# A gated mix of decode attention and a SwiGLU block: the last 128 rows of w_down loaded in two pieces instead of eight

## The chip, the cores and the metric

The kernel runs on one core of a Trainium2 chip. The metric is the device time of one execution in microseconds (us), lower is better; times given are medians of several runs on the same chip.

## The reference

One token x of 512 values goes through two blocks, and a gate mixes their results. All tensors are bf16.

```python
g = sigmoid((x * gate_w).sum(-1))
# A: attention of 32 query heads over 8 cached K/V heads of 32768 positions x 128
q = (x @ wq).reshape(32, 128)                       # wq: 512 x 4096
p = softmax(q . k_cache[head // 4] * 128 ** -0.5)   # k_cache, v_cache: 8 x 32768 x 128
a = (p . v_cache[head // 4]).reshape(4096) @ wo     # wo: 4096 x 512
# B: feed-forward
b = (silu(x @ w_gate) * (x @ w_up)) @ w_down        # 512 x 1792, 512 x 1792, 1792 x 512
out = g * a + (1 - g) * b
```

K and V are 64 MiB each, and every byte is read once; the weights are 14 MB together.

## The kernel before

Everything is loaded through one DMA queue, in the order in which SP issues it: wq, w_gate and w_up, then for each of the eight K/V heads (groups) its K of 8 MiB and, one group behind, its V, then w_down, then wo. `page` is a tile of five pages of 32 KB per partition in which these loads land; K alternates between pages 0 and 1 and pages 1 and 2, V takes pages 3 and 4, and the last V takes pages 1 and 2. A load into a page waits until PE has read what was there. `sem_fill` counts PE's transposed pieces of K, 16 to a group; `sem_v_free` counts groups whose V has been used.

PE runs `emit_start` (the projections, the gate, the feed-forward's hidden vector), then the main loop over the eight groups, then `emit_end`. In a group PE transposes K in 16 pieces into PSUM (L364), DVE copies each to `ktT` (L735), PE multiplies it by the group's queries (L376), DVE takes the maximum, ACT the exponentials (L619), and PE multiplies them by V (L433) for the group before.

The feed-forward's hidden vector of 1792 values is made in `emit_start`. It lies in `trow`, in four strips of 448 on partitions 0, 32, 64 and 96; DVE spreads it to `tmask`, where a column has one value that is not zero (L706), and PE turns columns of `tmask` into partitions by multiplying with ones (L541). The first 1664 values become `tT`, 128 partitions x 13, and the last 128 become `tX`, 32 partitions x 4. The rows of w_down lie the same way: `wd` has 13 rows on each partition, in one load (L345), and the last 128 rows go to the first 32 partitions of page 0, four rows of 1 KB on each, side by side. L351 loads these in eight DMAs (`XQ` = 8): DMA q fills partitions q, 8 + q, 16 + q and 24 + q, so that four DMA engines (`XE` = 4) get one descriptor of 4 KB each. Page 0 held K of the last group, so SP first waits for all of K to be transposed (L348). Then it waits for the V of the last group but one to be used (L352) and issues wo in five pieces, of 16, 9, 4, 2 and 1 rows on each partition (L356).

In `emit_end` PE uses the last V, reduces, multiplies `tT` with `wd` and `tX` with the extra rows (`emit_strip`, L232), and then takes wo's pieces as they land: the first by `emit_strip`, the others by `emit_rows` (L243). DVE makes one bf16 row of the result (L788), and SP and ACT store half of it each.

GpSimd's program makes ones and index rows at the start and then only passes on semaphores.

Of the kernel before, what the change touches and what calls it, by code (L numbers as in the profile page):

```python
# [6 lines left out]
ALU = mybir.AluOpType  # L7
AX = mybir.AxisListType
BF16 = mybir.dt.bfloat16
# [3 lines left out]
def bass_gated_mix__gqa_block_cached__swiglu_ffn__decode_kernel(  # L13
# [14 lines left out]
    G = A_k_cache.shape[1]  # L28
# [4 lines left out]
    F = B_w_gate.shape[1]  # L33
    NOUT = A_wo.shape[1]
# [3 lines left out]
    FC = F // 128  # L38
# [37 lines left out]
    assert G % 2 == 0  # L76
    PAD = 768

    XQ, XE, FX = 8, 4, 4
    XP = XQ * XE  # L80
    FM = FC - XP * FX // 128
    FR = 128 * FM
    assert FR + XP * FX == F and FX == NSTRIP

    with ExitStack() as es:
        def S_(name):
            return es.enter_context(nc.semaphore(name))
# [9 lines left out]
        sem_ld_g = S_("s_ld_g")  # L97
        sem_ld_wd = S_("s_ld_wd")
        sem_ld_wx = S_("s_ld_wx")
        sem_ones = S_("s_ones")  # L100
        sem_dc = S_("s_dc")
        sem_pz = S_("s_pz")
# [42 lines left out]
        def T(name, shape, dt):  # L145
            return es.enter_context(nc.sbuf_tensor(name, shape, dt))
# [15 lines left out]
        qblk = T("qblk", [128, (G + 2) * STEP], BF16)  # L162
        qcur = T("qcur", [128, 2, 2 * HPG], BF16)
        tT = T("tT", [128, FM], BF16)
        tX = T("tX", [XP, FX], BF16)
        pad = T("pad", [128, PAD // 2], BF16)
        page = T("page", [128, NPG, PAGE], BF16)
        wd = T("wd", [128, FM, NOUT], BF16)
# [53 lines left out]

        wq_v = page[:, PG_Q, 0 : KC * H * DH].rearrange("p (c n) -> p c n", c=KC)
        wgu = page[:, PG_F, 0 : 2 * KC * F].rearrange("p (w c f) -> p w c f", w=2, c=KC)
        wx = page[0:XP, PG_A, 0 : FX * NOUT]
        wx_v = wx.rearrange("p (i n) -> p i n", i=FX)
        wo_v = page[:, PG_X, 0 : WOJ * NOUT].rearrange("p (j n) -> p j n", j=WOJ)
        qall = qblk[:, :].rearrange("p (g e c) -> p g e c", e=2, c=2 * HPG)

# [42 lines left out]
        with nc.Block("main") as block:  # L272
            @block.gpsimd
            def _(pool):
                pool.memset(ones_f[:, :], 1.0).then_inc(sem_ones, 1)
                pool.memset(ones_bf[:, :], 1.0).then_inc(sem_ones, 1)
                pool.memset(r_row[:, 0, 0:1], 0.0).then_inc(sem_r, 1)
                n, k = 1, 1
                while n < 128:
                    pool.wait_ge(sem_r, k)  # L280
                    pool.tensor_scalar(
                        r_row[:, 0, n : 2 * n], r_row[:, 0, 0:n], float(n), None, op0=ALU.add
                    ).then_inc(sem_r, 1)
                    n *= 2
                    k += 1
                pool.wait_ge(sem_r, k)
                pool.tensor_scalar(
                    r_row[:, 1, :], r_row[:, 0, :], -1.0, None, op0=ALU.mult
                ).then_inc(sem_r, 1)
                for g in range(1, G):  # L290
                    pool.wait_ge(sem_k[1], 16 * g)
                    if g > 1:
                        pool.wait_ge(sem_k[0], 16 * (g + 1))
                    else:
                        pool.wait_ge(sem_k1, 16)
                    pool.sem_inc(sem_k[1], 16)

            @block.sync
            def _(sp):
                def load_k(g):  # L300
                    lo = PG_A if g % 2 else PG_B
                    dst = page[:, lo : lo + NB, :].rearrange("p b (r d) -> p b r d", d=DH)
                    src = A_k_cache[0, g, :, :].rearrange("(p b r) d -> p b r d", b=NB, r=R)
                    if g > 1:
                        sp.wait_ge(sem_fill, UPG * (g - 1) + UPP)
                        sp.dma_start(
                            dst.rearrange("p b r d -> p (b r d)"),
                            src.rearrange("p b r d -> p (b r d)"),
                        ).then_inc(sem_k[0], 16)
                        return  # L310
                    for b in range(NB):
                        first = lo + b == PG_B
                        if g and first:
                            sp.wait_ge(sem_fill, UPP)
                        sp.dma_start(dst[:, b, :, :], src[:, b, :, :]).then_inc(
                            sem_k[0] if first else sem_k1 if g else sem_k[1], 16
                        )

                def load_v(g):
                    src = A_v_cache[0, g, :, :].rearrange("(p b r) d -> p b r d", b=NB, r=R)  # L320
                    if g == G - 1:
                        lo, sem = PG_L, sem_vl
                        sp.wait_ge(sem_fill, UPG * g + UPP)
                    else:
                        lo, sem = PG_V, sem_v
                        if g:
                            sp.wait_ge(sem_v_free, STEP * (g + 1))
                        else:
                            sp.wait_ge(sem_pe_h, 1)
                    sp.dma_start(  # L330
                        page[:, lo : lo + NB, :].rearrange("p b n -> p (b n)"),
                        src.rearrange("p b r d -> p (b r d)"),
                    ).then_inc(sem, 16)

                sp.dma_start(wq_v, A_wq.rearrange("(p c) n -> p c n", c=KC)).then_inc(sem_q, 16)
                for w, src in enumerate((B_w_gate, B_w_up)):
                    sp.dma_start(
                        wgu[:, w, :, :], src.rearrange("(p c) f -> p c f", c=KC)
                    ).then_inc(sem_f, 16)
                load_k(0)  # L340
                for g in range(1, G):
                    load_k(g)
                    load_v(g - 1)
                load_v(G - 1)
                sp.dma_start(  # L345
                    wd[:, :, :], B_w_down[0:FR, :].rearrange("(p j) n -> p j n", j=FM)
                ).then_inc(sem_ld_wd, 16)
                sp.wait_ge(sem_fill, UPG * G)  # L348
                rest = B_w_down[FR:F, :].rearrange("(e q i) n -> q e (i n)", q=XQ, i=FX)
                for q in range(XQ):  # L350
                    sp.dma_start(wx[q:XP:XQ, :], rest[q]).then_inc(sem_ld_wx, 16)  # L351
                sp.wait_ge(sem_v_free, STEP * G)  # L352
                src = A_wo.rearrange("(p j) n -> p j n", j=WOJ)
                for k, s in enumerate(sem_wo):
                    a, b = WO_CUTS[k], WO_CUTS[k + 1]
                    sp.dma_start(wo_v[:, a:b, :], src[:, a:b, :]).then_inc(s, 16)  # L356

            @block.tensor
            def _(pe):
# [103 lines left out]
                def emit_start():  # L463
# [70 lines left out]
                                    skip_group_check=True,  # L534
                                )
                    ins.then_inc(sem_pe_h, 1)
                    pe.wait_ge(sem_dve_tm, 1)
                    for c, n, lo, hi, m in ((M_T0, FM, 0, FR, 128), (M_T0 + FM, FX, FR, F, XP)):
                        tv = tmask[:, lo:hi].rearrange("p (m j) -> p j m", j=n)
                        for j in range(n):  # L540
                            ins = pe.matmul(  # L541
                                ps_m[0:m, c + j : c + j + 1],
                                tv[:, j, :],
                                ones_bf[:, 0:1],
                                start=True,
                                stop=True,
                            )
                    ins.then_inc(sem_pe_t, 1)
                    pe.wait_ge(sem_ps0, 1)
                    pe.wait_ge(sem_dve_tT, 2)  # L550
                    for n, sem in enumerate((sem_v_free, sem_red)):
                        c = M_P0 + HPG * n
                        pe.matmul(  # L553
# [16 lines left out]
                def emit_end():  # L570
# [5 lines left out]
                    pe.wait_ge(sem_ld_wd, 16)  # L576
                    for j in range(FM):
                        emit_strip(pe, wd, tT, j, j < NSTRIP, False)
                    pe.wait_ge(sem_ld_wx, 16 * XQ)
                    for j in range(FX):  # L580
                        emit_strip(pe, wx_v, tX, j, False, False, at=FM)

                    pe.wait_ge(sem_dve_oT2, 1)
                    pe.matmul(
# [46 lines left out]
            def _(dve):  # L631
                ndc = [0]

                def dchain(ins):
                    ins.then_inc(sem_dc, 1)
                    ndc[0] += 1
                    dve.wait_ge(sem_dc, ndc[0])

                dchain(dve.memset(qblk[:, :], 0.0))
                for t in pst:  # L640
                    dve.memset(t[:, :], 0.0).then_inc(sem_pz, 1)
                dve.wait_ge(sem_pe_d, 1)
# [32 lines left out]
                for par in range(2):  # L675
# [27 lines left out]
                        ALU.mult,  # L703
                    )
                )
                dve.tensor_tensor(  # L706
                    tmask.rearrange("p (s f) -> p s f", s=NSTRIP),
                    trow.unsqueeze(1).to_broadcast([128, NSTRIP, FS]),
                    strip_sel.unsqueeze(2).to_broadcast([128, NSTRIP, FS]),
                    ALU.mult,  # L710
                ).then_inc(sem_dve_tm, 1)
                dve.wait_ge(sem_pe_t, 1)
                dve.tensor_copy(tT[:, :], ps_m[:, M_T0 : M_T0 + FM]).then_inc(sem_dve_tT, 1)
                dve.tensor_copy(
                    tX[:, :], ps_m[0:XP, M_T0 + FM : M_T0 + FM + FX]
                ).then_inc(sem_dve_tT, 1)

                def emit_out(i, at):
                    dve.wait_ge(sem_red, i + STEP)
# [101 lines left out]
```

## Time and profile before

| | us |
|---|---|
| median of 3 runs | 350.08 (349.88 to 350.38) |
| profiled execution | 349.81 |
| its span, first to last instruction | 348.5 |
| PE busy | 262.4 |
| DVE busy | 186.3 |
| ACT busy | 33.4 |
| GpSimd busy | 2.8 |
| bytes read, rate over the span | 148.11 MB, 425 GB/s |

In the profile, L12 is line 12 of the kernel above, "out<-in" names what an operation writes and reads, and a row's numbers in parentheses or behind an x are counts of instructions. A DMA share of 1 means that all sixteen engines had a transfer open the whole time; a transfer's bytes are counted where it starts, so that short stretches are rough. "The chain that ended last" is followed back from the last instruction to what released each step.

### The profile page before, as it was taken

Reading aid. Unit: us, or ns where it says so; the run is one execution under the profiler, and the core shown is the slowest. Engines: PE = TensorE matmul, PEld = TensorE weight load, DVE = VectorE, ACT = ScalarE, POOL = GpSimd, SP = SyncE. Lnnn points to the kernel's source line nnn. Section 1 sums busy time; section 2 is a strip of 40 time slices with the busy share of each in tenths; the row PEclk is TensorE's granted clock in tenths of the full one; section 3 lists DMA queues with packets and bytes.
Section 4 is the critical chain, followed back from the end, with each engine's and each line's share of the span. In section 5 each row is a group of like instructions: output and inputs, shape, how many; then the busy total and the mean of one; then the engine's idle time right before and its main releaser. Section 6 shows DMA issues by size and latency. Waiting matters only on the chain.

```text
span 348.5 us, 8862 instructions
## 1 busy us (share of the span) xinstructions
PE 262.4 (75%) x3921; PEld 222.3 (64%) x3921; DVE 186.3 (53%) x228; ACT 33.4 (10%) x143; POOL 2.8 (1%) x15
## 2 busy tenths in 40 slices
PE   1355996799859981999469992999379973999384
PEld 1125986699459941997269942996279843995241
DVE  4044885499239921697139911895149920894101
ACT  1002000300030003000400003000400012000400
POOL 3000000000000000000000000000000000000000
PEclk9975798699889986799859987998859995898678
DMA  8999999999999999999999999999999999999996
GB/s 311 428 463 421 419 427 466 461 406 436 421 444 451 414 436 421 459 436 414 436 436 451 429 414 436 436 451 429 414 444 451 429 436 414 444 459 414 392 396 266
DMA packets 3970, 148.21 MB, mean 425 GB/s; under 512 B 474, under 2 KB 604, under 8 KB 892
## 3 DMA queue, kind: packets, MB, share of 16 engines
q1 hardware_dynamic: 3956, 148.11, 98.7%
q8 instruction: 6, 0.10, 0.1%
q10 hardware_dynamic: 8, 0.00, 0.0%
HBM read 148.11 MB, written 0.00 MB: 425 GB/s over the span
## 4 chain that ended last, share of the span: by engine, by line
DMA 58%; PE 36%; DVE 3%; issue 2%; SPq 1%; ACT 0%; DVEq 0%
DMA page<-in_A_k_cache_dram 46%; PE pst L364 26%; DMA page<-in_A_wo_dram 6%; PE ps_sc L376 6%; DMA page<-in_B_w_up_dram 6%; PE ps_o L433 2%; DVE ktT L735 1%; PE pst L528 1%; DVE ktT L706 1%; SPq L356 0%; PE ps_m L541 0%; PE ps_m L553 0%; DVE pmaxf L743 0%; DVE ktT L697 0%; PE ps_sc L243 0%
## 5 line engine op out<-in xcount | busy, mean ns | idle before, releaser
L735 DVE COPY ktT<-pst 128x2048 bf16<-128x2048 bf16 x128 | 153.6, 1222 | 65.3 <-PE pst L364 60.9
L364 PE MATMUL pst<-ident_f,page 128*128 128x128 f32 x1024 | 149.7, 302 | 38.4 <-DMA page<-in_A_k_cache_dram 35.4
L364 PEld LDWEIGHTS pst<-ident_f,page 128*128 128x128 f32 x1024 | 128.6, 156 | 42.5 <-DMA page<-in_A_k_cache_dram 35.9
L376 PEld LDWEIGHTS ps_sc<-qcur,ktT 128*128 128x128 bf16 x2048 | 64.0, 97 | 7.9 <-DVE ktT L735 6.8
L376 PE MATMUL ps_sc<-qcur,ktT 128*128 128x8 bf16 x2048 | 64.3, 166 | 6.1 <-DVE ktT L735 6.1
L433 PE MATMUL ps_o<-page,ET 128*16 128x512 bf16 x512 | 38.9, 472 | 5.7 <-DMA page<-in_A_v_cache_dram 5.7
L433 PEld LDWEIGHTS ps_o<-page,ET 128*16 128x16 bf16 x512 | 14.5, 107 | 26.2 <-issue 18.8
L619 ACT ACTIVATE ET<-ps_sc,nbias 128x128 bf16 x64 | 23.9, 555 | 53.3 <-DVE nbias L761 53.3
L612 ACT ACTIVATE acc<-ps_o 128x512 f32<-128x512 f32 x8 | 4.8, 597 | 220.0 <-PE ps_o L433 215.7
L753 DVE TENSOR_REDUCE gm<-ps_m 4x1 f32<-4x128 f32 x8 | 2.2, 279 | 39.3 <-PE ps_m L413 39.3
L619 ACT ACTIVATION_READ_ACCUMULATOR ET<-ps_sc,nbias 128x1 f32 x64 | 18.2, 285 | 0.0
L743 DVE TENSOR_REDUCE pmaxf<-ps_sc 128x4 f32<-128x512 f32 x16 | 11.0, 687 | 8.4 <-PE ps_sc L376 8.4
L490 PE MATMUL pst<-page,xT 128*1 128x512 bf16 x32 | 3.6, 627 | 8.9 <-DMA page<-in_A_wq_dram 8.9
L454 PE MATMUL ps_m<-sel,acc 128*128 128x4 f32 x64 | 8.4, 255 | 1.8 <-ACT acc L612 1.6
L454 PEld LDWEIGHTS ps_m<-sel,acc 128*128 128x128 f32 x64 | 7.7, 191 | 2.5 <-ACT acc L612 2.2
L417 PE MATMUL ps_m<-diag,ones_f 4*128 4x4 f32 x16 | 3.2, 268 | 6.9 <-DVE diag L757 6.9
L720 DVE RECIPROCAL rS<-ps_m 128x4 f32<-128x4 f32 x9 | 1.6, 183 | 12.1 <-PE ps_m L454 12.1
L417 PEld LDWEIGHTS ps_m<-diag,ones_f 4*128 4x128 f32 x16 | 2.7, 213 | 8.4 <-issue 8.4
L490 PEld LDWEIGHTS pst<-page,xT 128*1 128x1 bf16 x32 | 1.0, 115 | 10.7 <-issue 10.7
L670 DVE CAST ktT<-pst 128x1024 bf16<-128x1024 f32 x2 | 2.4, 1220 | 8.4 <-PE pst L490 8.4
L445 PEld LDWEIGHTS ps_m<-esum,ones_f 128*128 128x128 f32 x32 | 4.2, 190 | 3.5 <-issue 3.5
L445 PE MATMUL ps_m<-esum,ones_f 128*128 128x4 f32 x32 | 4.9, 258 | 0.0
(73 smaller groups left out, 49.4 us busy)
## 6 DMA issues: line engine op xcount, KB each, us to landing
page<-in_A_k_cache_dram SPq DMA_DIRECT2D x4, 4096.0 KB, 34.8
page<-in_A_wq_dram SPq DMA_DIRECT2D x1, 4096.0 KB, 13.4
page<-in_A_wo_dram SPq DMA_DIRECT2D x1, 2048.0 KB, 18.4
page<-in_B_w_gate_dram SPq DMA_DIRECT2D x1, 1792.0 KB, 17.1
page<-in_B_w_up_dram SPq DMA_DIRECT2D x1, 1792.0 KB, 20.9
wd<-in_B_w_down_dram SPq DMA_DIRECT2D x1, 1664.0 KB, 31.3
page<-in_A_wo_dram SPq DMA_DIRECT2D x1, 1152.0 KB, 20.8
page<-in_A_wo_dram SPq DMA_DIRECT2D x1, 512.0 KB, 21.5
```

The source lines that it names most:

```text
L364: ins = pe.transpose(pst[u % NST][:, k * 128 : (k + 1) * 128], kv[:, n * 128 : (n + 1) * 128], ident_f[:, :],)
L376: ins = pe.matmul(ps_sc[b][:, col : col + 2 * HPG], kt[:, k, e, :], qcur[:, e, :], start=(e == 0), stop=(e == 1),)
L417: pe.matmul(ps_m[:, M_B0 : M_B0 + HPG], ones_f[0:HPG, :], diag[:, :], start=True, stop=True,).then_inc(sem_b, STEP)
L433: ins = pe.matmul(ps_o[32 * c : 32 * c + RQ * HPG, :], ET[:, n : n + RQ, :].rearrange("p n h -> p (n h)"), v[:, k * RQ : (k + 1) * RQ, :], ...
L445: pe.matmul(ps_m[:, M_S0 : M_S0 + HPG], ones_f[:, :], esum[:, b, :], start=(b == 0), stop=(b == NB - 1),)
L454: ins = pe.matmul(ps_m[:, M_P0 : M_P0 + HPG], acc[:, q, :], sel4[:, q * HPG : (q + 1) * HPG], start=(q == 0), stop=(q == RQ - 1),)
L490: ins = pe.matmul(pst[0][32 * k : 32 * k + 1, t * QN : (t + 1) * QN], xT[:, c : c + 1], wq_v[:, c, n : n + QN], start=(c == 0), stop=(c == ...
L528: ins = pe.matmul(pst[1][32 * k : 32 * k + 1, w * 512 : w * 512 + FS], xT[:, c : c + 1], wgu[:, w, c, k * FS : (k + 1) * FS], start=(c == ...
L612: act.activation(part, ps_o[:, :], ACT.Copy).then_inc(sem_acc, STEP)
L619: act.activation(ET[:, b * R : (b + 1) * R, h], sc[:, h, bass.ds(bank, R)], ACT.Exp, bias=nbias[:, h : h + 1], scale=SCALE, accum_out=esum ...
L735: dve.tensor_copy(ktT[:, n % NKT, :], pst[n % NST][:, :].bitcast(BF16)).then_inc(sem_cp, 1)
L743: dve.tensor_reduce(pmaxf[:, b, :], sc, AX.X, ALU.max).then_inc(sem_d, 1)
```

## The change

The last 128 rows go in two loads (`XH` = 2) of sixteen partitions each, 0 to 15 and 32 to 47. In load h, DMA engine e (of four) fills partitions 32h + 4e + q for q = 0 to 3, with rows of w_down that lie 16 KB apart, so that at each q the four engines read neighbouring 4 KB. Partitions 16 to 31 lie between the two halves, so GpSimd clears the first 48 partitions of the page before the loads (new semaphore `s_wz`, on which SP's loads wait in place of `sem_fill`), DVE clears `tX`, which has 48 partitions now, and the matmul runs over all 48. The values of the hidden vector must follow the rows: DVE writes the last 128 columns of `tmask` once more, in two products that reorder them, behind a wait for the first product; PE makes `tX` in eight matmuls instead of four, and DVE copies it in two parts instead of one.

```diff
@@ -76,11 +76,13 @@
     assert G % 2 == 0
     PAD = 768
 
-    XQ, XE, FX = 8, 4, 4
-    XP = XQ * XE
-    FM = FC - XP * FX // 128
+    XH, XE, XQ, FX = 2, 4, 4, 4
+    XP = XE * XQ
+    XS = 32 * (XH - 1) + XP
+    FM = FC - XH * XP * FX // 128
     FR = 128 * FM
-    assert FR + XP * FX == F and FX == NSTRIP
+    assert FR + XH * XP * FX == F
+    assert XH * XP * FX <= FS
 
     with ExitStack() as es:
         def S_(name):
@@ -97,6 +99,7 @@
         sem_ld_g = S_("s_ld_g")
         sem_ld_wd = S_("s_ld_wd")
         sem_ld_wx = S_("s_ld_wx")
+        sem_wz = S_("s_wz")
         sem_ones = S_("s_ones")
         sem_dc = S_("s_dc")
         sem_pz = S_("s_pz")
@@ -162,7 +165,7 @@
         qblk = T("qblk", [128, (G + 2) * STEP], BF16)
         qcur = T("qcur", [128, 2, 2 * HPG], BF16)
         tT = T("tT", [128, FM], BF16)
-        tX = T("tX", [XP, FX], BF16)
+        tX = T("tX", [XS, FX], BF16)
         pad = T("pad", [128, PAD // 2], BF16)
         page = T("page", [128, NPG, PAGE], BF16)
         wd = T("wd", [128, FM, NOUT], BF16)
@@ -222,8 +225,8 @@
 
         wq_v = page[:, PG_Q, 0 : KC * H * DH].rearrange("p (c n) -> p c n", c=KC)
         wgu = page[:, PG_F, 0 : 2 * KC * F].rearrange("p (w c f) -> p w c f", w=2, c=KC)
-        wx = page[0:XP, PG_A, 0 : FX * NOUT]
-        wx_v = wx.rearrange("p (i n) -> p i n", i=FX)
+        wz = page[0:XS, PG_A, 0 : FX * NOUT]
+        wx = [page[32 * h : 32 * h + XP, PG_A, 0 : FX * NOUT] for h in range(XH)]
         wo_v = page[:, PG_X, 0 : WOJ * NOUT].rearrange("p (j n) -> p j n", j=WOJ)
         qall = qblk[:, :].rearrange("p (g e c) -> p g e c", e=2, c=2 * HPG)
 
@@ -294,6 +297,8 @@
                     else:
                         pool.wait_ge(sem_k1, 16)
                     pool.sem_inc(sem_k[1], 16)
+                pool.wait_ge(sem_fill, UPG * G)
+                pool.memset(wz, 0.0).then_inc(sem_wz, 1)
 
             @block.sync
             def _(sp):
@@ -345,10 +350,12 @@
                 sp.dma_start(
                     wd[:, :, :], B_w_down[0:FR, :].rearrange("(p j) n -> p j n", j=FM)
                 ).then_inc(sem_ld_wd, 16)
-                sp.wait_ge(sem_fill, UPG * G)
-                rest = B_w_down[FR:F, :].rearrange("(e q i) n -> q e (i n)", q=XQ, i=FX)
-                for q in range(XQ):
-                    sp.dma_start(wx[q:XP:XQ, :], rest[q]).then_inc(sem_ld_wx, 16)
+                sp.wait_ge(sem_wz, 1)
+                rest = B_w_down[FR:F, :].rearrange(
+                    "(h q e i) n -> h e q (i n)", h=XH, q=XQ, e=XE
+                )
+                for h in range(XH):
+                    sp.dma_start(wx[h], rest[h]).then_inc(sem_ld_wx, 16)
                 sp.wait_ge(sem_v_free, STEP * G)
                 src = A_wo.rearrange("(p j) n -> p j n", j=WOJ)
                 for k, s in enumerate(sem_wo):
@@ -534,20 +541,26 @@
                                     skip_group_check=True,
                                 )
                     ins.then_inc(sem_pe_h, 1)
-                    pe.wait_ge(sem_dve_tm, 1)
-                    for c, n, lo, hi, m in ((M_T0, FM, 0, FR, 128), (M_T0 + FM, FX, FR, F, XP)):
-                        tv = tmask[:, lo:hi].rearrange("p (m j) -> p j m", j=n)
-                        for j in range(n):
+                    pe.wait_ge(sem_dve_tm, XH)
+                    tv = tmask[:, 0:FR].rearrange("p (m j) -> p j m", j=FM)
+                    tx = tmask[:, FR:F].rearrange(
+                        "p (h m i) -> p i h m", h=XH, m=XP
+                    )
+                    cols = [(tv[:, j, :], 128) for j in range(FM)]
+                    cols += [(tx[:, i, :, :], XP) for i in range(FX)]
+                    for j, (lhsT, m) in enumerate(cols):
+                        for h in range(1 if m == 128 else XH):
                             ins = pe.matmul(
-                                ps_m[0:m, c + j : c + j + 1],
-                                tv[:, j, :],
+                                ps_m[32 * h : 32 * h + m, M_T0 + j : M_T0 + j + 1],
+                                lhsT if m == 128 else lhsT[:, h, :],
                                 ones_bf[:, 0:1],
                                 start=True,
                                 stop=True,
+                                skip_group_check=True,
                             )
                     ins.then_inc(sem_pe_t, 1)
                     pe.wait_ge(sem_ps0, 1)
-                    pe.wait_ge(sem_dve_tT, 2)
+                    pe.wait_ge(sem_dve_tT, 1 + XH)
                     for n, sem in enumerate((sem_v_free, sem_red)):
                         c = M_P0 + HPG * n
                         pe.matmul(
@@ -576,9 +589,10 @@
                     pe.wait_ge(sem_ld_wd, 16)
                     for j in range(FM):
                         emit_strip(pe, wd, tT, j, j < NSTRIP, False)
-                    pe.wait_ge(sem_ld_wx, 16 * XQ)
+                    pe.wait_ge(sem_ld_wx, 16 * XH)
+                    w = wz.rearrange("p (i n) -> p i n", i=FX)
                     for j in range(FX):
-                        emit_strip(pe, wx_v, tX, j, False, False, at=FM)
+                        emit_strip(pe, w, tX, j, False, False, at=FM)
 
                     pe.wait_ge(sem_dve_oT2, 1)
                     pe.matmul(
@@ -637,6 +651,7 @@
                     dve.wait_ge(sem_dc, ndc[0])
 
                 dchain(dve.memset(qblk[:, :], 0.0))
+                dchain(dve.memset(tX[:, :], 0.0))
                 for t in pst:
                     dve.memset(t[:, :], 0.0).then_inc(sem_pz, 1)
                 dve.wait_ge(sem_pe_d, 1)
@@ -703,17 +718,32 @@
                         ALU.mult,
                     )
                 )
-                dve.tensor_tensor(
-                    tmask.rearrange("p (s f) -> p s f", s=NSTRIP),
-                    trow.unsqueeze(1).to_broadcast([128, NSTRIP, FS]),
-                    strip_sel.unsqueeze(2).to_broadcast([128, NSTRIP, FS]),
-                    ALU.mult,
-                ).then_inc(sem_dve_tm, 1)
+                dchain(
+                    dve.tensor_tensor(
+                        tmask.rearrange("p (s f) -> p s f", s=NSTRIP),
+                        trow.unsqueeze(1).to_broadcast([128, NSTRIP, FS]),
+                        strip_sel.unsqueeze(2).to_broadcast([128, NSTRIP, FS]),
+                        ALU.mult,
+                    )
+                )
+                n = XP * FX
+                for h in range(XH):
+                    lo = F - n * (XH - h)
+                    at = FS - n * (XH - h)
+                    dve.tensor_scalar(
+                        tmask[:, lo : lo + n].rearrange("p (e q i) -> p e q i", e=XE, q=XQ),
+                        trow[:, at : at + n].rearrange("p (q e i) -> p e q i", e=XE, q=XQ),
+                        strip_sel[:, NSTRIP - 1 : NSTRIP],
+                        None,
+                        op0=ALU.mult,
+                    ).then_inc(sem_dve_tm, 1)
                 dve.wait_ge(sem_pe_t, 1)
                 dve.tensor_copy(tT[:, :], ps_m[:, M_T0 : M_T0 + FM]).then_inc(sem_dve_tT, 1)
-                dve.tensor_copy(
-                    tX[:, :], ps_m[0:XP, M_T0 + FM : M_T0 + FM + FX]
-                ).then_inc(sem_dve_tT, 1)
+                for h in range(XH):
+                    at = slice(32 * h, 32 * h + XP)
+                    dve.tensor_copy(
+                        tX[at, :], ps_m[at, M_T0 + FM : M_T0 + FM + FX]
+                    ).then_inc(sem_dve_tT, 1)
 
                 def emit_out(i, at):
                     dve.wait_ge(sem_red, i + STEP)
```

## The prediction

> **What bounds the kernel now.** I read the transfer summary first, then the chain that ended last, then the rate by stretch, then what the queue's issuer (SP) waits for. The summary (packets, MB, share of sixteen DMA engines) says that the transfers never pause:
>
> ```profile
> q1 hardware_dynamic: 3956, 148.11, 98.7%
> ```
>
> The chain's end shows what the last part waits for. Columns: start, duration, what.
>
> ```profile
> 315.62 1.23 DVE ktT L735
> 316.89 0.96 PE ps_sc L376 x32
> 317.85 5.28 PE ps_o L433 x64
> ...
> 324.47 21.67 DMA page<-in_A_wo_dram
> 346.14 0.04 issue
> 346.18 0.64 PE ps_sc L243 x12
> 346.82 0.02 issue
> 346.84 0.29 DVE res_row L788
> ```
>
> The last piece of A_wo is issued at 324.47 and lands at 346.14; behind it stand 0.64 us of matmuls, one copy and the store. PE's work ahead of it is over long before. So the end comes when the DMA engines have drained their queue, and an edit counts only if it changes how long the draining takes, or leaves the queue empty for a while. The rate by stretch (columns: length, busy time of PE, PEld, DVE, ACT and POOL, PE clock, DMA share, GB/s):
>
> ```profile
> 300.00:324.00 24.00, 22.98 (x396) 19.04 (x392) 16.83 (x17) 0.60 (x1) 0.00 (x0) 0.93 1.00 434
> 331.00:334.00 3.00, 1.90 (x20) 0.77 (x24) 0.00 (x0) 0.00 (x0) 0.00 (x0) 0.50 0.97 414
> 334.00:337.00 3.00, 3.00 (x44) 1.21 (x40) 0.00 (x0) 0.00 (x0) 0.00 (x0) 0.75 1.02 339
> 337.00:344.00 7.00, 4.73 (x62) 2.42 (x54) 0.98 (x5) 1.20 (x2) 0.00 (x0) 1.00 0.98 414
> ```
>
> One stretch stands out. From 334 to 337 the share is full (1.02, packets are open all the time) and yet 339 GB/s arrive instead of 434. What passes then follows from the issues (line, operation, count, KB each, us to landing):
>
> ```profile
> wd<-in_B_w_down_dram SPq DMA_DIRECT2D x1, 1664.0 KB, 31.3
> page<-in_B_w_down_dram SPq DMA_DIRECT2D x8, 16.0 KB
> page<-in_A_wo_dram SPq DMA_DIRECT2D x1, 2048.0 KB, 18.4
> ...
> 305.42 0.43 SPq L345 DMA_DIRECT2D wd<-in_B_w_down_dram  x1
> 315.34 5.07 SPq L351 DMA_DIRECT2D page<-in_B_w_down_dram  x8
> 323.14 2.24 SPq L356 DMA_DIRECT2D page<-in_A_wo_dram  x5
> ```
>
> The bulk of w_down, issued right after the last V pages, lands 31.3 us after its issue at 305.42, so near 336.7. The eight small loads stand behind it on the same queue and ahead of A_wo. The slow stretch is where those eight loads run out and A_wo begins. Lost there are (434 - 339) x 3 = 285 KB, or 285 / 434 = 0.66 us; against the neighbours at 414 it is 225 KB, 0.54 us. Since everything afterwards waits for the draining, this is on the path in full.
>
> **The change part by part.** *The loads.* Removed: eight loads of 16 KB, each of four rows of 4 KB to partitions eight apart. Added: two of 64 KB, each of sixteen rows to neighbouring partitions, four in a row for each of the same four parts of the source. The bytes are the same, 131 KB, and so is the number of 4 KB rows, 32. Six completion signals on each engine in use go; the trace does not price one, and the eight loads together can cost no more than the stretch they lie in. What can change is the 0.54 to 0.66 us of stall. Its bounds: a gain of the whole of it, 0.66 (0.95 if the 414 after it, seven us long and (434 - 414) x 7 / 434 = 0.32 us short, is its tail and not the price of smaller rows), and, since the trace does not show the new shape, a loss of the same size or of twice that. I take the gain of 0.66: of all loads these are the only ones that send four short rows to partitions far apart, and the only stretch after the start in which a full queue moves a fifth less than 434 is theirs. [...]
>
> [...]
>
> *The clearing.* GpSimd writes 48 partitions x 2048 columns of bf16 once all K tiles are transposed, and SP's two loads wait for it.
>
> ```profile
> L275 POOL MEMSET ones_f<- x1: 205/205/205, 0.7 to 0.7; 128x128 f32 x1
> L276 POOL MEMSET ones_bf<- 128x2 bf16 x1 | 0.1, 97 | 0.0
> SPq L356 <- PE ps_o L433: 2.7, 1, 2.7
> ...
> 329.34 0.58 ACT L619 ACTIVATE ET<-ps_sc,nbias 128x128 bf16 x1
> 332.10 5.30 PE L433 MATMUL ps_o<-page,ET 128*16 128x512 bf16 x64 [5.65 <-DMA page<-in_A_v_cache_dram]
> ```
>
> From 2 columns in 97 ns to 128 in 205 ns is 0.86 ns a column: 2048 columns take 1.9 us, or 1.0 if two are cleared at once. It begins where SP's wait ended, at 315.3, and if the last tile copy (to 316.84) held it up, it ends by 318.8. Two issues at 5.07 / 8 = 0.63 each make 320.1. Behind SP's new wait stand these loads and then A_wo's five, and A_wo isn't issued before 323.14, for it waits for PE (the 2.7 us above). So the clearing costs nothing; even 3 us more would only delay issues whose data cannot move before 334. If instead it held up the tile copy for 1.9 us, PE's matmuls and the exponentials behind it would come 1.9 later; they end at 329.9 and V's data at 332.1 is what PE then waits for: 2.2 us of cover. Nothing.
>
> *The start.* tX's own memset and its wait lie ahead of DVE's idle time. After the masked product DVE adds a wait and two small products, PE four matmuls, DVE one copy:
>
> ```profile
> 27.86 2.02 DVE L706 TENSOR_TENSOR ktT<-ktT,ident 128x1792 bf16<-128x1792 bf16 x1
> 29.94 1.17 PE L541 MATMUL ps_m<-ones_bf,ktT 128*128 128x1 bf16 x17 [4.16 <-DVE ktT L706]
> 31.23 0.14 DVE L714 CAST tX<-ps_m 32x4 bf16<-32x4 f32 x1
> L648 DVE CAST pmat<-ident_f 128x128 bf16<-128x128 f32 x1 | 0.3, 261 | 0.0
> L690 DVE TENSOR_SCALAR og_col<-g_col 128x1 f32<-128x1 f32 x1 | 0.1, 149 | 0.0
> ```
>
> A product over 64 columns lies between 149 ns (one column) and 261 ns (128 columns, reordered); two make 0.30 to 0.52, I take 0.40. PE: 4 x 1.17 / 17 = 0.28. The copy: 0.08 to 0.14. Together 0.8 us later into the main loop. The chain that ended last runs from here on PE and DVE up to 76.42, where K for group 2 is issued, so that issue comes 0.8 later:
>
> ```profile
> 76.42 23.80 DMA page<-in_A_k_cache_dram
> page<-in_A_wq_dram SPq DMA_DIRECT2D x1, 4096.0 KB, 13.4
> 4.00:20.00 16.00, 5.34 (x42) 2.55 (x42) 4.40 (x9) 0.17 (x1) 0.00 (x0) 1.00 0.98 419
> PE pst L364 <- DMA page<-in_A_k_cache_dram: 35.4, 6, 7.1
> ```
>
> In the first row 23.8 us pass from issue to landing of 8.39 MB, which need 8.39 / 0.434 = 19.3. So 4.5 us were queueing and start-up. The first load of all met an empty queue, and took 13.4 us for 4.19 MB, 10.0 at 419: start-up is at most 3.4. The queue therefore held 1.1 to 4.5 us of other work when this load was issued, and 0.8 fits below the lower bound. From the next group on PE waits for K itself (35.4 us in six waits), which swallows the shift. Cost nothing; with the cover gone it would be up to 0.8.
>
> *The end.* The same four matmuls take w_down's rest, now over 48 rows, and whatever they add lies ahead of a wait for A_wo of 1.09 us:
>
> ```profile
> 341.69 1.03 PE L232 MATMUL ps_sc<-page,O 128*1 128x512 bf16 x16 [1.09 <-DMA page<-in_A_wo_dram]
> ```
>
> Nothing.
>
> **Sum.** The profiled execution took 349.81 us, 348.5 of span and 1.3 around it; the median of the runs shown is 350.08, 0.27 above. 349.81 - 0.66 + 0 + 0 + 0 = 349.15; on the median's scale 349.4.
>
> **The rivals.** *Stall stays (B).* It would belong to the passage from w_down to A_wo, as all sixteen engines begin rows that are 32 KB apart. For it: such a beginning is slow once more, at the start of wq. Against it: the later pieces of A_wo have the same spacing and run at 414.
>
> ```profile
> 1.50:4.00 2.50, 0.00 (x0) 0.00 (x0) 1.57 (x2) 1.28 (x1) 1.99 (x7) 1.00 1.09 341
> ```
>
> Then nothing changes but a few signals: 350.0.
>
> *Stall grows (C), the slower side.* Each load now goes to sixteen partitions only, and each part of the source is read in 4 KB pieces 16 KB apart, where the eight old loads walked through 32 KB in order. If crowding at either side is what stalls, the place is the same stretch, 334 to 337, and the price another 0.66 (350.7) to 1.3 (351.4), middle 351.1; it counts as slower from a stall of 1.36 us on. Against it: the same 32 partitions' worth of rows and the same four sources at a time. [...]
>
> *The start's cover is too thin (D).* Should the queue hold less than the added 0.8 us at 76.4, the engines idle for the rest, at most 0.8: 350.9. Against it stands the lower bound of 1.1.
>
> **How the numbers follow.** About 0.2%, 0.7 us, is what a measurement of this kernel tells from no change. Forecast (A) 0.48, B 0.26, C 0.16, D 0.10. A runs from a gain of 0.54 to one of 0.95, so a bit over half of it, 0.28, lies beyond 0.7; with 0.02 of B faster is 0.30. Same: 0.20 of A, 0.22 of B, 0.02 each of C and D: 0.46. Slower: 0.14 of C, 0.08 of D, 0.02 of B: 0.24. With the spread of the runs A's own range is 349.0 to 349.7. The range 349.0 to 350.9 takes in A, B, D and C's lower end, and leaves out some 0.15.
>
> **What would show it.** In the changed profile: the stretch 334 to 337 at 414 or more; A_wo's last piece landing near 345.5 instead of 346.14 with the same 2.4 us behind it; SP's two issues done before 321 and A_wo's first issue still near 323; the loop's first transposes 0.8 us later, and K for group 2 landing within 0.3 us of 100.2. I am wrong if the slow stretch keeps its depth (B), deepens (C), or if it is gone and the time stays, which would mean that another engine's queue ended last.

## The result and the profile after

The changed kernel takes 349.19 us (349.06 to 349.53, 13 runs) against 349.96 (349.70 to 350.38, 13 runs): a ratio of 0.9978, with a 95% interval of 0.9969 to 0.9986, or 0.77 us less. Its profiled execution took 349.16, with a span of 347.8 (before: 349.81 and 348.5).

The rate by stretch of the changed kernel, in the same stretches as before:

```profile
331.00:334.00 3.00, 1.79 (x20) 0.75 (x24) 0.00 (x0) 0.00 (x0) 0.00 (x0) 0.50 0.95 408
334.00:337.00 3.00, 3.00 (x44) 1.21 (x40) 0.00 (x0) 0.00 (x0) 0.00 (x0) 0.65 1.02 435
337.00:344.00 7.00, 5.50 (x94) 2.83 (x90) 0.98 (x5) 1.20 (x2) 0.00 (x0) 1.00 0.98 413
```

The slow stretch is gone: 435 GB/s where it was 339, at the same full share of 1.02. Its neighbours are near where they were (408 and 413 instead of 414). The chain that ended last (start, duration, what) has moved by as much:

```profile
315.93 1.22 DVE ktT L765
317.20 0.96 PE ps_sc L383 x32
318.16 5.28 PE ps_o L440 x64
...
324.78 20.75 DMA page<-in_A_wo_dram
345.53 0.04 issue
345.57 0.29 PE ps_sc L246 x8
345.87 0.04 issue
345.90 0.27 PE ps_sc L246 x4
346.17 0.02 issue
346.19 0.29 DVE res_row L818
```

PE's steps around 317 are 0.31 us later than before and wo's last piece is issued 0.31 later, yet it lands 0.61 earlier, at 345.53 instead of 346.14. What follows the landing takes 2.3 us instead of 2.4. The timeline shows the clearing and the two loads:

```profile
315.69 1.80 POOL L301 MEMSET page<- 48x2048 bf16 x1 [311.70 <-PE pst L371]
317.52 1.48 SPq L358 DMA_DIRECT2D page<-in_B_w_down_dram  x2
323.45 2.24 SPq L363 DMA_DIRECT2D page<-in_A_wo_dram  x5
```

### The profile page after: what moved, and what is told of

It is laid out like the page before. It is cut to its first block, busy times and chain, and to the rows that moved or that the text cites. A ratio compares the mean times of both kernels' runs of the same rounds, so it can differ in the third digit from the quotient of the medians.

```text
span 347.8 us, 8869 instructions
## 1 busy us (share of the span) xinstructions
PE 260.8 (75%) x3925; PEld 220.6 (63%) x3925; DVE 186.6 (54%) x232; ACT 33.4 (10%) x143; POOL 4.6 (1%) x16
## 4 chain that ended last, share of the span: by engine, by line
DMA 64%; PE 33%; DVE 2%; issue 1%; SPq 1%; ACT 0%; DVEq 0%
DMA page<-in_A_k_cache_dram 52%; PE pst L371 24%; DMA page<-in_B_w_up_dram 6%; DMA page<-in_A_wo_dram 6%; PE ps_sc L383 5%; PE ps_o L440 2%; PE pst L535 1%; DVE ktT L722 1%; DVE ktT L765 0%; SPq L363 0%; PE ps_m L553 0%; PE ps_m L566 0%; DVE ktT L712 0%; DVE ktT L710 0%; PE ps_sc L246 0%
## 5 line engine op out<-in xcount | busy, mean ns | idle before, releaser
L371 PE MATMUL pst<-ident_f,page 128*128 128x128 f32 x1024 | 147.2, 299 | 39.5 <-DMA page<-in_A_k_cache_dram 38.2
L371 PEld LDWEIGHTS pst<-ident_f,page 128*128 128x128 f32 x1024 | 126.0, 154 | 43.9 <-DMA page<-in_A_k_cache_dram 38.8
L301 POOL MEMSET page<- 48x2048 bf16 x1 | 1.8, 1798 | 311.7 <-PE pst L371 311.7
```

The costliest lines, as they stand in the source:

```text
L371: ins = pe.transpose(pst[u % NST][:, k * 128 : (k + 1) * 128], kv[:, n * 128 : (n + 1) * 128], ident_f[:, :],)
```

## The experiments

Three sides of the new loads had to be told apart from each other and from the rest of the change: the loads are fewer (theory N), their source is read in another order (S), and they go to other partitions (P). All kernels are the changed one with a few lines edited, except one that is named; each is compared with the kernel before on the same chip. The pieces of code leave out the semaphores. A ratio is estimated from all executions of a kernel, so where these lie far apart it need not be that of the medians; a rate is that of one profiled execution.

**The eight old loads in the changed kernel.**

```diff
-rest = B_w_down[FR:F, :].rearrange("(h q e i) n -> h e q (i n)", h=XH, q=XQ, e=XE)
-for h in range(XH):
-    sp.dma_start(wx[h], rest[h])
+rest = B_w_down[FR:F, :].rearrange("(e q i) n -> q e (i n)", q=8, i=FX)
+for q in range(8):
+    sp.dma_start(page[q:32:8, PG_A, 0 : FX * NOUT], rest[q])
```

> The changed kernel with the eight old loads put back (four rows each, to partitions q, 8+q, 16+q, 24+q; its extra rows of w_down then stand on other partitions than the hidden vector's values). If the whole gain lies in the loads: about 349.96, ratio to before 1.000 (0.999 to 1.001), and 334 to 337 us back at about 340 GB/s. If the gain comes from another part of the change (the start, the clearing, where the clock or the code lies): ratio 0.998 and 334 to 337 at 430 or more.

Measured: 349.97, ratio 0.9999 (0.9990 to 1.0008). Its rate by stretch:

```profile
334.00:337.00 3.00, 3.00 (x36) 1.08 (x32) 0.00 (x0) 0.00 (x0) 0.00 (x0) 0.50 1.04 337
```

The whole gain lies in the loads; with the start, the clearing and the extra matmuls kept, the time is that of the kernel before (349.97 against 349.98 on the same chip).

**Eight loads to the new places.**

```diff
 for h in range(XH):
-    sp.dma_start(wx[h], rest[h])
+    for q in range(XQ):
+        sp.dma_start(wx[h][q:XP:XQ, :], rest[h, :, q, :])
```

> The changed kernel with its two loads cut into eight, of four rows each, every row to the same partition as in the changed kernel and from the same place. Theories P and S: no stall, ratio 0.998 (some 0.04 us of signals more), 334 to 337 at 425 or more. Theory N: the stall is back, ratio 1.000, 334 to 337 near 340.

Measured: 349.15, ratio 0.9978 (0.9969 to 0.9987), the same as the changed kernel (349.19, ratio 0.9978); the 0.04 us put for signals is not seen.

```profile
334.00:337.00 3.00, 3.00 (x32) 1.07 (x28) 0.00 (x0) 0.00 (x0) 0.00 (x0) 0.50 1.04 442
```

Theory N falls: eight loads of four rows, each row at the new place, took 349.15, two of sixteen 349.19.

**The source in plain order.**

```diff
-"(h q e i) n -> h e q (i n)"
+"(h e q i) n -> h e q (i n)"
```

> The changed kernel with the source taken in plain order: engine e reads 16 KB in one piece, the four engines 16 KB apart, as the old loads did with 32 KB (the rows then stand on other partitions than their values). Theories P and N: no stall, ratio 0.998, 334 to 337 at 430 or more. Theory S: the stall is back at least in part, ratio 0.999 to 1.000, 334 to 337 below 400.

Measured: 350.63, ratio 1.0021 (1.0012 to 1.0030), slower than before, as no theory said. The page's count of packets tells that more than the order had changed. Of the changed kernel and of this one:

```profile
DMA packets 3946, 148.21 MB, mean 426 GB/s; under 512 B 450, under 2 KB 580, under 8 KB 868
```

```profile
DMA packets 3971, 148.21 MB, mean 424 GB/s; under 512 B 475, under 2 KB 605, under 8 KB 893
```

The changed kernel has 450 packets under 512 B with two loads of these rows, the kernel before 474 with eight, and so has the kernel with the eight loads to the new places: 24 packets for six loads, four for each. Here there are 475 with two loads, one of them on a queue of its own (q14), so 24 more for the same two loads, sixteen for each. The author takes these packets for completion signals, one for each engine that a load uses: four engines there, sixteen here. No record names the engines. By the author's guess, rows that follow each other in memory had become one dimension of sixteen, and each of sixteen engines got one row of each load, for one of the same sixteen partitions. Its rate sinks to 294 GB/s from 334 to 337; in shorter stretches, whose shares show how rough they are, it sinks twice:

```profile
334.00:335.50 1.50, 1.50 (x20) 0.58 (x16) 0.00 (x0) 0.00 (x0) 0.00 (x0) 0.50 1.08 277
335.50:336.50 1.00, 1.00 (x16) 0.34 (x12) 0.00 (x0) 0.00 (x0) 0.00 (x0) 0.50 1.54 433
336.50:338.00 1.50, 1.50 (x26) 0.57 (x18) 0.00 (x0) 0.00 (x0) 0.00 (x0) 0.95 0.59 229
```

So this run says nothing on S. It does say that two loads of the same bytes to the same partitions, by sixteen engines as the packets are read here, took 350.63, 1.4 us more than by four.

**The source 32 KB apart, still by four engines.**

```diff
-"(h q e i) n -> h e q (i n)"
+"(e h q i) n -> h e q (i n)"
```

> The changed kernel with the source read as the old eight loads read it, each of the four engines going through 32 KB in order and the four 32 KB apart, but still by four engines (in the run with the source in plain order the records show every one of the sixteen engines with two of the 4 KB rows, so it told of the number of engines as well); the rows then stand on other partitions than their values. Theory P, the place: no stall, ratio 0.998, 334 to 337 at 430 or more. Theory S, the source: the stall is back, ratio 0.9995 to 1.001, 334 to 337 at 350 or less.

Measured: 349.15, ratio 0.9973 (0.9964 to 0.9982).

```profile
334.00:337.00 3.00, 3.00 (x49) 1.19 (x41) 0.00 (x0) 0.00 (x0) 0.00 (x0) 0.87 1.02 435
```

Theory S falls: read in the old way and written in the new places, the rows pass at 435 GB/s. What is left is the place.

**The two loads to other partitions.** The loop and the source stay; only the destination of load h changes, in four ways. The matmul still reads the old places, so that these rows, or half of them, are left out of the result:

```diff
-sp.dma_start(wx[h], rest[h])                       # 0 to 15, 32 to 47
+page[32 * h + 16 : 32 * h + 32, ...]               # 16 to 31, 48 to 63
+page[64 + 32 * h : 64 + 32 * h + 16, ...]          # 64 to 79, 96 to 111
+page[16 * h : 16 * h + 16, ...]                    # 0 to 15, 16 to 31
+page[32 * h + 4 : 32 * h + 20, ...]                # 4 to 19, 36 to 51
```

16 to 31 and 48 to 63:

> The changed kernel with its two loads sent to partitions 16 to 31 and 48 to 63 instead of 0 to 15 and 32 to 47 (the matmul reads the old place, so these rows are left out of the result). Theory P, the place: an engine's rows must lie in the partitions that it also fills in a 128-partition load; here all four engines write to another's, so the stall is back, as deep as before or deeper: ratio 1.000 or above, 334 to 337 at 350 GB/s or less. Theory N, the number: two loads stall less than eight: ratio 0.998, 430 or more. Theory S, the source: rows next to each other in memory are read without a stall: ratio 0.998.

64 to 79 and 96 to 111:

> [...] Theory P1 and P2: as at 16 to 31 and 48 to 63, ratio 1.001 to 1.005, 334 to 337 below 300 GB/s. If the stall belonged to partitions 16 to 31 and 48 to 63 and not to their being another's: ratio 0.998, 334 to 337 at 430.

0 to 15 and 16 to 31:

> The changed kernel with the first load left at partitions 0 to 15 and the second sent to 16 to 31 (the matmul reads the old place, so half of these rows are left out of the result). Theory P: half of the foreign bytes of the run with 16 to 31 and 48 to 63, so a stall between none and that one's, ratio 0.999 to 1.002, 334 to 337 at 330 to 400. If a stall needs more foreign bytes than this to build up: ratio 0.998. Theory S: no stall, 0.998.

4 to 19 and 36 to 51:

> [...] Theory P1, what counts is bytes in the place of an engine that writes there at the same time: 32 KB, a quarter of the 128 KB of the run at 16 to 31 and 48 to 63, whose fastest execution was 1.36 us above the changed kernel: 0.2 to 0.5 us above it, ratio 0.9983 to 0.9992. Theory P2, every byte outside an engine's own place counts: 1.3 us and more above, ratio 1.001 to 1.004.

| destination | median, us | lowest and highest | ratio (95%) | GB/s, 334 to 337 |
|---|---|---|---|---|
| 0-15, 32-47 (changed kernel) | 349.19 | 349.06, 349.53 | 0.9978 (0.9969 to 0.9986) | 435 |
| 4-19, 36-51 | 349.73 | 349.50, 349.86 | 0.9993 (0.9984 to 1.0002) | 408 |
| 0-15, 16-31 | 350.48 | 349.71, 351.75 | 1.0014 (1.0002 to 1.0026) | 358 |
| 64-79, 96-111 | 350.56 | 350.17, 351.76 | 1.0030 (1.0019 to 1.0041) | 300 |
| 16-31, 48-63 | 351.44 | 350.53, 352.25 | 1.0040 (1.0028 to 1.0052) | 281 |

With nothing but the partitions changed, the time goes from 349.2 to 351.4. The executions behind the rates took 349.16, 349.73, 349.75, 350.26 and 352.25 us, so in the last three lines they are not the median ones. The profile's rows of the second and the last line:

```profile
334.00:337.00 3.00, 3.00 (x48) 1.11 (x40) 0.00 (x0) 0.00 (x0) 0.00 (x0) 0.80 1.00 408
```

```profile
334.00:337.00 3.00, 3.00 (x36) 1.11 (x28) 0.00 (x0) 0.00 (x0) 0.00 (x0) 0.50 1.04 281
```

The first is of the loads at 4 to 19 and 36 to 51, the second of those at 16 to 31 and 48 to 63. Which partitions an engine fills in a load of 128 no row shows, so theory P can only be held against the changed kernel's own places, 0 to 15 and 32 to 47, where the rate is 435 GB/s. Outside these 32 partitions lies none of the 128 KB in the first line of the table, 32 KB in the second (16 to 19 and 48 to 51), 64 KB in the third and all 128 KB in the last two. The eight old loads put 64 KB there as well (16 to 31), at 337 GB/s; their median of 349.97 lies below the third line's 350.48, their lowest time, 349.70, beside its 349.71. In the table the order of the times follows the bytes outside, by the medians and by the lowest times. That fits theory P1, with its 32 KB; P2, by which all 128 KB of the second line count, wanted 1.3 us and more above the changed kernel, and 0.54 was measured. P1's own size for it, 0.2 to 0.5, is just missed, and bytes and time are not in proportion. The profiles don't name engines, so the place itself is shown; that it is another engine's is the author's reading, and so is the division among engines in P1 and P2.

**Without the last rows.** The remaining runs ask whether the four engines that carry the extra rows are the ones that end last. Here the two loads are left out, and with them these rows of the result.

> The changed kernel without its two loads of the last 128 rows, which are left out of the result. If the four engines have 32 KB of room before the last of the others ends (theory of the balance): 0.0 to 0.1 us faster than the changed kernel, ratio 0.9975 to 0.9980. If the rows are on the path: 1.2 us faster, ratio 0.9943 to 0.9950.

Measured: 349.21, ratio 0.9979 (0.9970 to 0.9988). At 0 to 15 and 32 to 47 the 128 KB cost nothing that can be measured (349.19 with them), so, as the author reads it, the four engines that carry them are not alone in ending last: others, without these rows, end as late. No row shows when an engine ends.

**All rows in the bulk load** (the kernel before, with 14 rows of w_down on each partition and neither `tX` nor the eight loads).

> The kernel before with all 1792 rows of w_down in the one bulk load, 14 on each partition, and nothing left over: no extra loads, no stall, nothing left out. All sixteen engines get 8 KB more and four of them 32 KB less. If engines without the extra rows end as late as the four (theory of the balance), the end comes 8 KB later, 0.3 us, than in the changed kernel: 349.5, ratio 0.9985 to 0.9990. If the four end last by themselves: ratio 0.9965 to 0.9980.

Measured: 350.68, ratio 1.0017 (1.0008 to 1.0026), slower than both answers. Its slow stretch is gone (437 GB/s from 334 to 337), but another wait has come in at the start. K for group 2, issue and time to landing, from the timeline and the issues of this kernel:

```profile
78.50 0.33 SPq L300 DMA_DIRECT2D page<-in_A_k_cache_dram  x1
```

```profile
page<-in_A_k_cache_dram SPq DMA_DIRECT2D x1, 22.8
```

It is issued at 78.50 and lands near 101.3; in the kernel before it landed near 100.2, in the changed one near 100.3. PE's waits from 30 to 80 us (in total, times, longest) show part of why it was late, of this kernel and of the changed one:

```profile
PE ps_m L403 <- issue: 3.3, 1, 3.3
PE pst L354 <- issue: 2.9, 1, 2.9
```

```profile
PE pst L371 <- issue: 0.3, 1, 0.3
```

In 6.2 us PE waited for nothing that the profile shows. This profile is of an execution of 351.16 us, the longest of eleven and 2.0 above that of the changed kernel (349.16). By the author's estimate the late K can account for 1.0 of that (101.3 against 100.3), the 8 KB on every engine for the 0.3 that was expected (131 KB at 434 GB/s), and the remaining 0.7 has no cause here. Whether the other executions waited as long at the start is not shown, and there is no run with that wait removed, so this run does not decide between its two answers.

**Eight engines instead of four, and twice the rows on them.**

```diff
-XH, XE, XQ, FX = 2, 4, 4, 4
+XH, XE, XQ, FX = 1, 8, 4, 4     # 16 KB on each of eight engines
+XH, XE, XQ, FX = 2, 8, 4, 4     # 256 rows, 32 KB on each of eight
```

> The changed kernel with its rows on eight engines instead of four, 16 KB each, in one load to partitions 0 to 31 (engine e to 4e to 4e+3); nothing is left out, and no partitions lie between. Theory P: no stall, for each engine keeps to its own place. If the four engines with the rows are the ones that end last: 0.3 to 0.6 us faster than the changed kernel, ratio 0.9960 to 0.9970. If others, without such rows, end as late: ratio 0.9975 to 0.9980. If engines 4 to 7 are themselves late ones: 0.6 us slower than the changed kernel, ratio 0.9995.

> 256 rows instead of 128 go to the eight engines, 32 KB each, in two loads to partitions 0 to 31 and 32 to 63, and the bulk load has 12 rows on each partition instead of 13, which takes 8 KB from every engine; nothing is left out. Theory P: no stall. If the late engines are among the other eight: they end 8 KB sooner, 0.3 us, ratio 0.9968 to 0.9972. If some of engines 4 to 7 are late: 0.9 us slower than the changed kernel, ratio 1.000 or above.

Measured: 349.63 (349.10 to 351.34), ratio 0.9987 (0.9978 to 0.9996), and 349.90 (348.88 to 351.66), ratio 1.0002 (0.9992 to 1.0013). Neither stalls: 440 and 459 GB/s from 334 to 337, though 64 KB of the first and 128 KB of the second go to 16 to 31 and 48 to 63, where the rate with 128 KB from four engines was 281 GB/s. So these partitions are not slow by themselves. The first lies between its second and third answer, the second meets its second answer ("1.000 or above"), which would make some of engines 4 to 7 late ones; but their executions differ by more than 2 us, so they don't settle it. The first one's profile is of its longest execution, 351.34. There K for group 2 is issued at 77.32, again with PE's "issue" waits ahead of it:

```profile
PE pst L371 <- issue: 4.0, 2, 2.5
PE ps_m L420 <- issue: 2.6, 1, 2.6
```

No version beat the changed kernel clearly.

## Why the prediction was right, and where its steps were not

*The stall.* The forecast rested on 0.66 us of lost transfer between 334 and 337, all of it on the path, and on its going with the eight loads. The stretch went from 339 to 435 GB/s, and the old loads bring the stall and the time back. That step held, in mechanism and in size: in the profiled executions 0.65 us is gained, 0.61 of it at wo's landing. The medians differ by 0.77. The forecast of 349.4 is 0.2 above the measured median, and 0.12 of that is its starting point, 350.08 from three runs, where thirteen gave 349.96. The 414 behind the stretch was not its tail; it is 413 now. (The upper end of A, 0.95, is meant as 0.66 and 0.32, which make 0.98; nothing hangs on it.) The limit of 0.7 us for telling a change from none was wide: the interval of the ratio is 0.0009 to each side, 0.3 us, so a gain of 0.66 would have been told from none.

*The reason given for it* fell in part. That the stretch belongs to these loads held (337 GB/s with the old ones in the changed kernel, 435 with the new). That four short rows go to partitions far apart is not what counts: in eight loads of four rows each, four partitions apart, to the new places, nothing stalls (442 GB/s). And two loads of neighbouring rows, sent to 16 to 31 and 48 to 63, lose 1.4 us against the kernel before, where the same reason would have forecast the same gain of 0.66. That this change sends its loads to the right place is therefore, as far as that reason goes, luck. The place is what counts: with all 128 KB at 16 to 31 and 48 to 63, the rate of the whole core fell to 281 GB/s. Why it does was not shown; no row shows a write that is held up.

*Rival B*, the passage to A_wo as the cause, is out: the passage is still there and runs at 435 GB/s. *Rival C* is out for this change: its 0.66 to 1.3 us more for sixteen partitions at a time do not hold for the changed kernel, which writes to sixteen at a time and is 0.77 faster. Where, by the packets, sixteen engines were sent to the same sixteen partitions, the rate fell to 294 GB/s and 1.4 us were lost against the changed kernel, which would fit the crowding that C supposed; no row shows it.

*The clearing:* 1.80 us against 1.9, the two loads issued by 319.0, A_wo's first issue at 323.45. As forecast; the tile copy beside it was not held up either (1.22 us, as in the other groups).

*The start:* the main loop begins 0.52 us later (32.95 instead of 32.43) and not 0.8. The two products took 0.39, as forecast, but PE's 21 matmuls took 1.13, less than its 17 before (1.17), where 0.28 more was put; the extra copy cost about 0.2 instead of 0.1.

*K for group 2* is the step that failed: it was to be issued 0.8 later and came 3.0 earlier, at 73.44. From the start of the main loop to that issue PE does the same work in both kernels. Here is that stretch before, then changed, with the columns of the rate by stretch:

```profile
32.43:76.42 43.99, 38.33 (x540) 37.06 (x540) 30.48 (x32) 3.34 (x17) 0.00 (x0) 0.81 1.01 435
32.95:73.44 40.49, 35.90 (x540) 34.45 (x540) 30.29 (x32) 3.34 (x17) 0.00 (x0) 0.88 1.02 438
```

Of the 3.5 us less, 2.4 are PE's busy time, at a granted clock of 0.88 instead of 0.81, and 1.1 its waits: those put down to "issue" shrank from 2.9 to 0.3, while waits for DVE and K grew. The prediction had taken clock and waits as fixed. These are single executions, and what sets their clocks and waits apart is not shown. That the early issue gained nothing is because K then waited in the queue: it took 26.8 us to land instead of 23.8, and landed near 100.2 in both. The lower bound on the cover, 1.1 us from 76.42 on, is neither confirmed nor refuted. With the issue 2.1 us later, in the kernel with all rows in bulk, K landed 1.0 later, as the bound would have it; in the profile with eight engines the issue was only 0.9 later, and K took 24.5 us and landed near 101.8, 1.6 later. So *rival D* was no idle fear, only not this change's.

## What to carry to other kernels

When the DMA queue ends last, look for a stretch in which the share of open transfers is full and the rate is low: its loss tells about how much there is to gain, as 0.66 us did here. What slows it has to be found by experiment. For a small load cut four ways, try other destination partitions: here the same 128 KB took the kernel from 349.19 us (0 to 15, 32 to 47) to 351.44 (16 to 31, 48 to 63). Cutting it into eight loads, or reading its source 32 KB apart, made no difference here (349.15 both); taking the source in plain order made it 350.63, and there the count of small packets gave it away (475 instead of 450). Before calling a delay at the start hidden, measure how long the queue could have lasted, since PE's clock and waits that the profile gives no cause for can move that margin by more than the edit does: by 3 us here.

## What was not expected of the hardware

In one profiled execution rows outside 0 to 15 and 32 to 47 left a trace after they had passed. With the loads at 16 to 31 and 48 to 63, its rate did not recover until the end, though every later load went to its usual place:

```profile
337.00:346.00 9.00, 5.97 (x77) 2.83 (x66) 0.98 (x5) 1.19 (x2) 0.00 (x0) 0.88 0.99 340
```

This execution took 352.25 us, the longest of six (350.53 to 352.25). In the profiles with the loads at 0 to 15 and 16 to 31 and at 64 to 79 and 96 to 111, which took 349.75 and 350.26, the rate had recovered: 417 and 416 GB/s from 337 to 344, where this one has 343 and the changed kernel 413. The executions of these two kernels spread as widely, up to 351.8, while those of the changed kernel lie within 0.5 us; but single executions near 351.5 also came with rows on eight engines (351.34 and 351.66), whose profiles, of the executions of 351.34 and 349.90, show no stall from 334 to 337. Why the rate stayed low here, and whether the other long executions are of this kind, is open; no experiment was made on it.
